# Regrouping the projection matmuls inside the slots of a sliding-window attention kernel

## The chip, the cores and the metric

The kernel runs on one core of a Trainium2 chip. The metric is the device time of one execution in microseconds (us). The core has five engines that run their own instruction streams and meet by semaphores: TensorE (PE in the profile, with its weight loads as PEld), VectorE (DVE), ScalarE (ACT), GpSimd (POOL) and SyncE (SP), which here issues the transfers. TensorE writes only PSUM, a small memory of banks with 512 floats per partition.

## The reference

Everything is float32, with 2048 tokens of width 512.

```python
xn = layernorm(x)
q, k, v = heads(xn @ wqkv)                      # 32 heads of 16
scores = q @ k.T * 16 ** -0.5                   # each query sees itself and the 255 keys before it
s = softmax(where(mask, scores, -1e9)) @ v @ wo
y = layernorm(xn)
g = silu(gelu(y @ w1 + b1) @ w2 + b2)           # 512 -> 1792 -> 512
out = x + s * g
```

## The kernel before

Numbers of full float32 precision are split into a high and a low part, and a product is made of three matmuls (`PASSES`: high by high, high by low, low by high).

The attention is a loop over *slots*, t = 0 to 127. The 32 heads form eight groups n of four heads, and a slot handles one block of 128 tokens of one group: n = t // 16, block t % 16. Each slot issues the following, and every engine keeps this order (`Ordered`; the order is written out by hand in the last loop of `mixer_kernel`, and no scheduler changes it):

1. `prob_block(..., 1)`: the scores of two of the four heads, two matmuls that run side by side on the two halves of TensorE's rows, into the PSUM tile `stb`. ScalarE then makes exp of them (`pt<-stb`), and GpSimd cuts out the window with two selects.
2. `max_block` for the block that lies `LEAD` = 12 slots ahead (m = t + 12): four matmuls into the tile `xy`, with the keys of the block before and of the block itself; VectorE puts in place of the masked part the scores with the keys two blocks back (`copy_predicated`, which reads `zo`), and takes the row maximum (`mt<-xy`). Those scores with the keys two blocks back are `first_scores`, four small matmuls into `zo`. They are made at the end of the slot before, unless `max_block` is told that they are not made ahead; it then makes them itself, straight after its own four.
3. *fills of the first half* (`fill_in(t, 0)`), then whatever `plan` has for the slot.
4. `prob_block(..., 0)`: the scores of the other two heads, again into `stb`. So `stb` has to be read by the exp of step 1 before these may start, and by the exp of step 4 before the next slot may start.
5. *fills of the second half* (`fill_in(t, 1)`), then `first_scores` of block m + 1 (none in slots with t % 16 = 3 or 4, since the first two blocks of a group have no keys two blocks back).
6. `pv_step` of the block before: 24 small matmuls with the probabilities of three blocks (8 in slots with t % 16 = 1, 16 in those with t % 16 = 2), into `zo`, and ScalarE's copy of the result, `oraw<-zo`.

From slot 116 on there is no block ahead, so steps 2 and the `first_scores` are gone, and step 1 writes `xy` in place of `stb`.

The *fills* are matmuls of other stages, put between the scores: the projection to q and k of the next group (`pair_qk`), to v (`pair_v`), and the hidden layer of the MLP (`pair_h`). `tandem(t0, t1, one, two, mid, back)` spreads two such jobs over the slots t0 to t1. A job is n units (12, or 24 half as long ones for `pair_v`); one unit of a *pair of fills* is one matmul on the upper 64 rows and one on the lower 64 rows, side by side, into the two banks `fb[0]` and `fb[1]`. The units go through the n steps twice: in phase 0 (slots t0 to mid - 1) the banks take one half of the rows, in phase 1 (from mid, or `back`, on) they change rows. At that change, the first pair of phase 1 is made to wait for the newest `oraw` copy (`add_manual_dep`). In slot t1 the last three units come, and the two banks are copied out: bank 0 by ScalarE, bank 1 by VectorE (`pjr<-fb`, `vt<-fb`, `hr<-fb`); the next tandem begins in the slot after.

`places` inside `tandem` says how many of a slot's units go in its first half: `ahead`, at most a third of n (four pairs), or half of the slot's units. `BEHIND` lists eight slots t1 in which ScalarE's copy of bank 0 comes in the second half, behind the second exp.

After the copies of a projection come the split (ScalarE casts the high part, GpSimd subtracts) and six transfers per job to the tiles `qk`, from which the scores are made (`send_high`, `send_low`, line 43 like all issued work, since one helper records every operation).

Of the kernel before, what the change touches and what calls it, by code (L numbers as in the profile page):

```python
# [23 lines left out]
NQ = H // 4  # L24
EPS = 1e-5
NEG = -3.0e38
LEAD = 12
# [23 lines left out]
def mixer_kernel(ctx, tc, x, wqk, wv, wo, w1, b1, w2, b2, out):  # L51


    nc = SimpleNamespace(**{name: Ordered(tc, name) for name in ("tensor", "vector", "scalar", "gpsimd", "sync")})
# [22 lines left out]
    def load(pool, tag, src, name, shape=(P, 512)):  # L77
        t = pool.tile(list(shape), F32, tag=tag, name=name)
        nc.sync.dma_start(t, src)
        return t  # L80
# [79 lines left out]
    def run(steps):  # L160
        for step in steps:
            step()
# [13 lines left out]
    def open_slot(i):  # L176
        slots.append(bigp.tile([P, 2, 2, S], F32R, tag=f"qk{i}", name=f"qk{i}"))
# [18 lines left out]
    fb = [psf.tile([P, 512], F32, name=f"fb{i}") for i in range(2)]  # L196
# [90 lines left out]
    now = [0, 0]  # L287
    delayed = {}
    fills = {}

    def later(k, fn):

        if k == 0:
            fn()
        else:
            h = 2 * now[0] + now[1] + k
            delayed.setdefault((h // 2, h % 2), []).append(fn)
# [137 lines left out]
                behind(t, nc.sync.dma_start, h_d[f - 6], raw)  # L435
        return 3 * KT, mm, finish

    BEHIND = (19, 24, 35, 41, 58, 74, 90, 104)

    def tandem(t0, t1, one, two, mid=None, back=None):  # L440

        n = one[0]
        lo, hi = slice(0, 64), slice(64, P)
        mid = mid or max(1, (t0 + t1 + 1) // 2)
        most = n // 4

        def places(slots, last):

            last = min(most, n // (len(slots) + 1)) if last else 0
            cuts = [(n - last) * k // len(slots) for k in range(len(slots) + 1)]
            out = []
            for t, a, b in zip(slots, cuts, cuts[1:]):
                ahead = min(b - a, max(n // 3, (b - a + 1) // 2))
                out += [(t, 0)] * ahead + [(t, 1)] * (b - a - ahead)
            return out + [(t1, 0)] * last

        first, second = places(range(t0, mid), False), places(range(back or mid, t1), True)
        for phase, where in enumerate((first, second)):  # L460
            for i in range(n):
                flags = dict(start=(phase == 0 and i == 0), stop=(phase == 1 and i == n - 1), skip_group_check=True)
                def unit(i=i, phase=phase, flags=flags):
                    made = ((two if phase == 0 else one)[1](fb[1 - phase], i, hi, **flags),
                            (one if phase == 0 else two)[1](fb[phase], i, lo, **flags))
                    if phase == 1 and i == 0:
                        for r in made:
                            tc.add_manual_dep(r.ins, outs["copy"].ins.name, ORDER, reason="the banks change rows")
                fills.setdefault(where[i], []).append((unit, ()))
        fills.setdefault((t1, int(t1 in BEHIND)), []).append((one[2], (fb[0], t1, nc.scalar.copy)))  # L470
        fills[t1, 0].append((two[2], (fb[1], t1, nc.vector.tensor_copy)))

    def spread(jobs, places):
# [13 lines left out]
    def first_scores(n, qb):  # L487

        slot = slots[n % 2]
        for p in range(2):  # L490
            for a in (1, 0):
                r = slice(64 * a, 64 * a + 64)
                nc.tensor.matmul(zo[:, a, P * p: P * (p + 1)], slot[r, 0, p, P * qb: P * (qb + 1)],
                                 slot[r, 1, p, P * (qb - 2): P * (qb - 1)], start=True, stop=True)

    def max_block(n, qb, ahead=False):

        slot = slots[n % 2]
        if qb % 4 == 0:
            mts[n, qb // 4] = small.tile([P, 2, 2, 4], F32, tag="mt", name=f"mt_{n}_{qb}")  # L500
        lo = max(qb - 1, 0)
        off = 128 * (lo + 1 - qb)
        for p in range(2):
            for a in (1, 0):
                r = slice(64 * a, 64 * a + 64)
                nc.tensor.matmul(xy[:, a, 256 * p + off: 256 * (p + 1)], slot[r, 0, p, P * qb: P * (qb + 1)],
                                 slot[r, 1, p, P * lo: P * (qb + 1)], start=True, stop=True)
        if qb >= 2 and not ahead:
            first_scores(n, qb)
        four = xy.rearrange("q a (p k) -> q a p k", p=2)  # L510
        nc.vector.copy_predicated(four[:, :, :, 128:256], mask,
                                  neg if qb < 2 else zo[:, :, 0:256].rearrange("q a (p k) -> q a p k", p=2))
        nc.vector.tensor_reduce(out=mts[n, qb // 4][:, :, :, qb % 4],
                                in_=four[:, :, :, off:256],
                                axis=AX.X, op=ALU.max, negate=True)
# [32 lines left out]
    def prob_block(n, kb, p):  # L548
        slot = slots[n % 2]
        w = min(384, S - P * kb)  # L550
        pt = pp.tile([P, 2, 384], F32, tag="pt", name=f"pt_{n}_{kb}_{p}")
        both = xy if p and 16 * n + kb + LEAD >= 16 * NQ else stb[0]
        for a in (1, 0):
            r = slice(64 * a, 64 * a + 64)
            nc.tensor.matmul(both[:, a, 0:w], slot[r, 1, p, P * kb: P * (kb + 1)],
                             slot[r, 0, p, P * kb: P * kb + w], start=True, stop=True)
        nc.scalar.activation(pt[:, :, 0:w], both[:, :, 0:w], AF.Exp, scale=DH ** -0.5)
        nc.gpsimd.affine_select(out=pt[:, :, 0:P], in_=pt[:, :, 0:P], pattern=[[0, 2], [1, P]],
                                compare_op=ALU.is_ge, fill=0.0, base=0, channel_multiplier=-1)
        if w == 384:  # L560
            nc.gpsimd.affine_select(out=pt[:, :, 256:384], in_=pt[:, :, 256:384],
                                    pattern=[[0, 2], [-1, P]], compare_op=ALU.is_gt, fill=0.0,
                                    base=0, channel_multiplier=1)
        pts[(n, kb, p)] = pt
# [100 lines left out]
    def at(t, fn, *args):  # L665
        plan.setdefault(t, []).append((fn, args))
# [8 lines left out]
    ahead = load(pp, "pt", x[512: 640, :], "x_1_0")  # L675
# [28 lines left out]
    n, raw = raws["qk"]  # L704
# [32 lines left out]
    fills[0, 1].insert(0, fills[0, 0].pop())  # L737
    soon = {}
    tandem(3, 8, pair_qk(1, 2), pair_qk(1, 3))
    for n, spans in enumerate((((9, 14), (15, 19)), ((20, 24), (25, 30)), ((31, 35), (36, 41)), ((42, 47), (48, 53, 51)),  # L740
                               ((75, 79), (80, 84)), ((85, 90), (93, 98))), 2):
        for c, span in zip((0, 2), spans):
            tandem(*span[:2], pair_qk(n, c), pair_qk(n, c + 1), *span[2:])
    for i, (t0, t1) in enumerate(((54, 58), (59, 63), (64, 68), (69, 74))):
        tandem(t0, t1, pair_v(2 * i), pair_v(2 * i + 1))
# [66 lines left out]
    def fill_in(t, half):  # L812
        now[:] = t, half
        run(delayed.pop((t, half), ()))
        for fn, args in fills.get((t, half), ()):
            fn(*args)

    end = 16 * NQ
    for t in range(-16, end + 1):
        m = t + LEAD  # L820
        if t == -5:
            open_slot(1)
            for k in range(4):
                at(-4 + k, clear_part, k)
        if 0 <= t < end:
            if t == 0:
                early.close()
                stb.append(attn.enter_context(tc.tile_pool(name="ps_s2", bufs=1, space=PSUM)).tile(
                    [P, 2, 512], F32, name="stb"))
            prob_block(t // 16, t % 16, 1)  # L830
        if t >= 0 and m < end:
            max_block(m // 16, m % 16, t > 0)
        fill_in(t, 0)
        for fn, args in plan.get(t, []):
            fn(*args)
        if 4 <= m < LEAD:
            max_block(0, m)
        if 0 <= t < end:
            prob_block(t // 16, t % 16, 0)
        fill_in(t, 1)  # L840
        if 0 <= m < 4:
            max_block(0, m)
        if t >= 0 and m + 1 < end and (m + 1) % 16 >= 2:
            first_scores((m + 1) // 16, (m + 1) % 16)
        if t >= 1:
            pv_step((t - 1) // 16, (t - 1) % 16)
        run(lns.get(t, ()))
        if 0 <= m < end and m % 4 == 3:
            max_rows(m // 16, m % 16 // 4, t)
        for fn, args in ends.get(t, []):  # L850
            fn(*args)
# [22 lines left out]
    for f in range(6, NF, 2):  # L874
        t = gp.tile([P, 2, 512], F32, tag="ohl", name=f"hr_{f}", bufs=4)
# [429 lines left out]
```

## Time and profile before

| | |
|---|---|
| median of three runs | 753.11 us (752.19 to 753.17) |
| the profiled execution | 751.99 us |
| its span, first to last instruction | 750.3 us |
| TensorE busy | 735.8 us, 98% of the span |
| VectorE, ScalarE, GpSimd busy | 511.3, 439.5, 299.1 us |
| granted TensorE clock | 0.999 |
| slots 0 to 115 | from 62.0 to 398.4 us |
| slots 116 to 127 | from 398.4 to 427 us |

The timeline view gives one row for each run of like instructions on an engine: start, duration from the first start to the last end, engine, operation, what is written and read, how many, and in brackets the idle time before it and who ended it. Durations of matmuls overlap: the next matmul starts before the one before has left the array, so the time that a matmul takes from TensorE is read from start to start. A slot begins at the first matmul of `stb` of step 1; its first half ends at the start of the second pair on `stb`, and its second half at the next slot's first.

### The profile page before, as it was taken

The page shows a single profiled execution, that of the slowest core. Times are in us where ns is not written, and L with a number is a line of the kernel's source. Part 1 is how long each engine was busy: PE and PEld are TensorE (multiplying, and loading weights), DVE is VectorE, ACT ScalarE, POOL GpSimd, SP SyncE. Part 2 cuts the span into 40 slices and gives each one's busy share as a digit, 9 for nine tenths or more (in the row PEclk, how much of TensorE's full clock was granted, in tenths as well). Part 3 has the DMA queues.
Part 4 walks back from the last instruction along what each step waited for, and adds up shares of the span by engine and source line. Part 5 has one row for each costly group of instructions (what it writes and reads, how often), then busy time and mean ns, then how long its engine had stood idle before and what let it go on. Part 6 is the DMA issues. An engine that isn't in the chain of part 4 may idle for free.

```text
span 750.3 us, 18757 instructions
## 1 busy us (share of the span) xinstructions
PE 735.8 (98%) x7408; PEld 589.3 (79%) x7408; DVE 511.3 (68%) x781; ACT 439.5 (59%) x746; POOL 299.1 (40%) x644
## 2 busy tenths in 40 slices
PE   8999999999999999999999999999999999999997
PEld 7886777777778887777776688888888888888886
DVE  7886767877766778887772547763666765676643
ACT  7757767867667676778877745544453743442001
POOL 7413757767666555767866600120102000001102
PEclk9999999999999999999999999999999999999999
DMA  8633355766555535647734482542013332254711
GB/s 287 191 74 78 84 132 148 210 153 187 150 142 148 143 93 139 168 109 189 200 86 146 120 294 92 177 147 78 35 43 98 94 103 71 70 167 129 214 53 56
DMA packets 56951, 99.40 MB, mean 132 GB/s; under 512 B 11104, under 2 KB 11360, under 8 KB 56864
## 3 DMA queue, kind: packets, MB, share of 16 engines
q1 hardware_dynamic: 56864, 98.21, 46.0%
q8 instruction: 58, 0.95, 0.5%
q14 instruction: 29, 0.24, 0.1%
HBM read 51.39 MB, written 29.62 MB: 108 GB/s over the span
## 4 chain that ended last, share of the span: by engine, by line
PE 90%; ACT 4%; DVE 3%; DMA 1%; issue 1%; POOL 0%; SPq 0%; DVEq 0%; ACTq 0%
PE acc L43 20%; PE fb L43 19%; PE zo L43 12%; PE stb L43 9%; PE p L43 9%; PE s L43 6%; PE h L43 6%; PE xy L43 5%; PE pv L43 3%; ACT pt L43 3%; DVE xy L43 1%; PE yt L43 1%; DVE mt L43 1%; DMA qk<-pjr 0%; DMA x<-in_x_dram 0%
## 5 line engine op out<-in xcount | busy, mean ns | idle before, releaser
L43 POOL TENSOR_SCALAR_AFFINE_SELECT pt<-pt 128x256 f32<-128x256 f32 x480 | 193.7, 427 | 134.2 <-ACT pt L43 131.9
L43 ACT ACTIVATE pt<-stb 128x768 f32<-128x768 f32 (+1 forms) x244 | 188.4, 772 | 58.4 <-PE stb L43 51.7
L43 DVE TENSOR_REDUCE mt<-xy 128x4 f32<-128x1024 f32 (+1 forms) x128 | 152.6, 1192 | 4.4
L43 DVE COPY_PREDICATED xy<-upper,zo 128x512 f32<-128x512 int32 x112 | 77.8, 694 | 71.5 <-PE xy L43 64.9
L43 PE MATMUL fb<-xnT,wqb 64*128 64x512 f32 (+1 forms) x684 | 106.9, 398 | 0.3
L43 POOL TENSOR_TENSOR xo<-xo,gated 128x512 f32<-128x512 f32 x15 | 20.3, 1354 | 216.6 <-DVE gated L43 191.5
L43 PE MATMUL zo<-pt,vt 128*17 128x128 f32 x2880 | 103.7, 275 | 0.1
L43 PE MATMUL stb<-qk 64*128 64x384 f32 (+1 forms) x488 | 98.9, 401 | 4.5 <-ACT pt L43 2.8
L43 PE MATMUL acc<-w,gh 128*128 128x512 f32 x320 | 98.9, 390 | 0.0
L43 PEld LDWEIGHTS stb<-qk 64*128 64x128 f32 x488 | 45.5, 183 | 53.3 <-ACT pt L43 45.1
L43 PEld LDWEIGHTS zo<-pt,vt 128*17 128x17 f32 x2880 | 67.5, 97 | 15.2 <-issue 6.5
L43 PEld LDWEIGHTS fb<-xnT,wqb 64*128 64x128 f32 (+1 forms) x684 | 64.2, 185 | 10.0 <-DVE pjr L43 1.1
L43 PEld LDWEIGHTS acc<-w,gh 128*128 128x128 f32 x320 | 59.8, 188 | 12.1
L43 PE MATMUL acc<-w,gl 128*128 128x512 f32 x160 | 62.4, 390 | 0.0
L43 PE MATMUL xy<-qk 64*128 64x256 f32 (+2 forms) x536 | 58.3, 291 | 0.2 <-DVE mt L43 0.2
L43 ACT COPY oraw<-zo 128x128 f32<-128x128 f32 x128 | 34.2, 267 | 35.9 <-PE zo L43 34.8
L43 PEld LDWEIGHTS xy<-qk 64*128 64x128 f32 x536 | 46.8, 185 | 6.5 <-issue 3.1
L43 ACT ACTIVATE gated<-acc 128x512 f32<-128x512 f32 x16 | 8.7, 596 | 64.8 <-DVE acc L43 64.8
L43 PE MATMUL s<-wos,ohl 128*128 128x512 f32 (+1 forms) x204 | 44.7, 377 | 0.0
L43 PEld LDWEIGHTS zo<-qk 64*128 64x128 f32 x448 | 38.4, 185 | 6.0 <-issue 2.5
L43 PEld LDWEIGHTS s<-wos,ohl 128*128 128x128 f32 x204 | 36.7, 188 | 7.0
L43 ACT COPY p<-p 128x512 f32<-128x512 f32 x21 | 12.3, 584 | 49.5 <-PE p L43 42.2
(195 smaller groups left out, 1243.2 us busy)
## 6 DMA issues: line engine op xcount, KB each, us to landing
qk<-sh SPq DMA_DIRECT2D x128, 128.0 KB
qk<-pjr SPq DMA_DIRECT2D x64, 128.0 KB
oT_d<-oraw SPq DMA_DIRECT2D x32, 256.0 KB
w_d<-in_w_dram SPq DMA_DIRECT2D x14, 512.0 KB
x<-in_x_dram SPq DMA_DIRECT2D x16, 256.0 KB
or<-oT_d SPq DMA_DIRECT2D x16, 256.0 KB
w<-rden_d SPq DMA_DIRECT2D x16, 256.0 KB
xo<-in_x_dram SPq DMA_DIRECT2D x16, 256.0 KB
```

Of the source, the lines that this page charges most:

```text
L43: r = issue(*args, **kwargs)
```

## The change

Four edits to the order of work; no arithmetic, no tile and no transfer is added or removed.

- `places`: before slot 116, up to 5n/12 units of a slot (five pairs, or ten of the half-length units) go into its first half, whatever number the slot has. From slot 116 on it is a quarter of n (three), or half of the slot's units.
- The wait at the change of rows is not made in tandems that begin in slot 116 or later. There are two of them, which change rows in slots 119 and 125.
- `BEHIND` is gone: ScalarE's copy of bank 0 always comes in the first half of slot t1, ahead of the second exp, and its tiles are taken before those of VectorE's copy.
- `IN_PLACE`: the `first_scores` of the blocks m = 12 and m = 24 are made within `max_block`, in slots 0 and 12. For m = 12 that was so before (`t > 0` was false in slot 0); for m = 24 they move from the end of slot 11 to the first half of slot 12.

```diff
@@ -287,6 +287,7 @@
     fills = {}
+    IN_PLACE = (LEAD, 24)
@@ -435,8 +436,6 @@
-    BEHIND = (19, 24, 35, 41, 58, 74, 90, 104)
-
     def tandem(t0, t1, one, two, mid=None, back=None):
@@ -452,7 +451,7 @@
             for t, a, b in zip(slots, cuts, cuts[1:]):
-                ahead = min(b - a, max(n // 3, (b - a + 1) // 2))
+                ahead = min(b - a, 5 * n // 12) if t < 16 * NQ - LEAD else min(b - a, max(most, (b - a + 1) // 2))
                 out += [(t, 0)] * ahead + [(t, 1)] * (b - a - ahead)
@@ -463,11 +462,11 @@
-                    if phase == 1 and i == 0:
+                    if phase == 1 and i == 0 and t0 < 16 * NQ - LEAD:
                         for r in made:
                             tc.add_manual_dep(r.ins, outs["copy"].ins.name, ORDER, reason="the banks change rows")
                 fills.setdefault(where[i], []).append((unit, ()))
-        fills.setdefault((t1, int(t1 in BEHIND)), []).append((one[2], (fb[0], t1, nc.scalar.copy)))
+        fills.setdefault((t1, 0), []).append((one[2], (fb[0], t1, nc.scalar.copy)))
         fills[t1, 0].append((two[2], (fb[1], t1, nc.vector.tensor_copy)))
@@ -829,7 +828,7 @@
         if t >= 0 and m < end:
-            max_block(m // 16, m % 16, t > 0)
+            max_block(m // 16, m % 16, m not in IN_PLACE)
@@ -840,7 +839,7 @@
-        if t >= 0 and m + 1 < end and (m + 1) % 16 >= 2:
+        if t >= 0 and m + 1 < end and (m + 1) % 16 >= 2 and m + 1 not in IN_PLACE:
             first_scores((m + 1) // 16, (m + 1) % 16)
```

## The prediction

> **What bounds the kernel now.** I began with the page: TensorE is busy for 98% of the span, the others for 68% and less. Then the waits, to see what breaks into TensorE's stream.
>
> ```profile
> span 750.3 us, 18757 instructions
> PE 735.8 (98%) x7408; PEld 589.3 (79%) x7408; DVE 511.3 (68%) x781; ACT 439.5 (59%) x746; POOL 299.1 (40%) x644
> ...
> PEld stb L43 <- ACT pt L43: 45.1, 161, 0.7
> ```
>
> The last row says that the weight load for a score pair (`stb`) waits for ScalarE's exp 161 times. There is one tile `stb` and two exps per slot, so a slot has two lower bounds side by side: TensorE's own work, and the loop score, exp, score. The timeline of slot 13, which has four pairs of fills in its first half and one in its second (4+1), shows both.
>
> ```profile
> 100.84 0.44 PE L43 MATMUL stb<-qk 64*128 64x384 f32 x2
> 101.12 0.39 PE L43 MATMUL xy<-qk 64*128 64x256 f32 x4
> 101.35 1.09 PE L43 MATMUL fb<-xnT,wqb 64*128 64x512 f32 x8
> 102.28 0.43 PE L43 MATMUL stb<-qk 64*128 64x384 f32 x2
> 102.55 0.39 PE L43 MATMUL fb<-xnT,wqb 64*128 64x512 f32 x2
> ...
> 103.83 0.39 PE L43 MATMUL stb<-qk 64*128 64x256 f32 x2
> ...
> 102.76 0.81 ACT L43 ACTIVATE pt<-stb 128x768 f32<-128x768 f32 x1 [0.54 <-PE stb L43]
> ```
>
> Read from start to start: a score pair takes 0.28 us (100.84 to 101.12), four pairs of fills 0.93 (101.35 to 102.28), so a pair 0.235. The slot takes 2.99: a first half of 1.44 and a second of 1.55. The second exp ends at 103.57, 0.26 before the next slot, so this second half is TensorE's. It is not so in slot 18, also 4+1, where `pv_step` has 16 matmuls in place of 24:
>
> ```profile
> 115.78 0.44 PE L43 MATMUL stb<-qk 64*128 64x384 f32 x2 [0.39 <-ACT pt L43]
> 117.21 0.42 PE L43 MATMUL stb<-qk 64*128 64x384 f32 x2
> 118.54 0.46 PE L43 MATMUL stb<-qk 64*128 64x384 f32 x2
> ```
>
> It takes 2.76, with halves of 1.43 and 1.33: its fifth pair costs nothing, since it lies under the exp.
>
> **The change, part by part. Five pairs in the first half.** I worked the cuts of `places` through for all tandems. Before slot 116, 42 slots change: 4+1 becomes 5+0, 4+2 becomes 5+1, and some `pair_v` slots gain half a pair. With a fifth pair the first half is TensorE's: 0.51 up to the first fill (100.84 to 101.35) and five times 0.235, 1.69. What the second half becomes needs a slot in which the first exp is done long before the second score. Slot 42 (4+0) is one, because its fills began late:
>
> ```profile
> 184.98 0.45 PE L43 MATMUL stb<-qk 64*128 64x384 f32 x2
> ...
> 186.61 0.33 PE L43 MATMUL stb<-qk 64*128 64x384 f32 x2
> 186.78 0.33 PE L43 MATMUL zo<-qk 64*128 64x128 f32 x4
> ...
> 187.85 0.45 PE L43 MATMUL stb<-qk 64*128 64x384 f32 x2
> ...
> 186.41 0.19 PEld L43 LDWEIGHTS stb<-qk 64*128 64x128 f32 x2
> ...
> 186.99 0.81 ACT L43 ACTIVATE pt<-stb 128x768 f32<-128x768 f32 x1 [0.63 <-PE stb L43]
> ```
>
> The weight load of the score starts at 186.41, 0.20 before its matmul, under the last fills. So the pair takes 0.17 (186.61 to 186.78) and not 0.28, its exp starts 0.38 behind it and not 0.48, and the second half is 1.24, which is now the least a second half with a full exp can have (0.38 + 0.81 + 0.05 to the next score).
>
> - *Slots like 13* (7, 13, 23, 40, 89, 103, 109): 2.99 becomes 1.69 + 1.24 = 2.93. With the slots a little shorter than 13, 0.05 each, -0.35 for seven. Slot 29, of the same kind, I leave at 0.
> - *Slots like 18*, whose second half was already the exp's (18, 34, 52, 83, 97, 114, and 65 and 81, which have 4+2 but 8 matmuls of `pv_step`): 2.76 becomes 2.93, +0.17 each, +1.36 for eight. Two slots of `pair_v` (66, 67) move half a pair; by slot 18's price I estimate +0.1 each: +0.2.
> - *4+2 becoming 5+1*, slot 16:
>
> ```profile
> 109.82 0.44 PE L43 MATMUL stb<-qk 64*128 64x384 f32 x2
> ...
> 111.28 0.40 PE L43 MATMUL stb<-qk 64*128 64x384 f32 x2
> 111.52 0.63 PE L43 MATMUL fb<-xnT,wqb 64*128 64x512 f32 x4
> ...
> 113.03 0.44 PE L43 MATMUL stb<-qk 64*128 64x384 f32 x2
> ```
>
> TensorE's work binds both halves and the pair only moves; what is gained is the rest of the load, 0.24 (111.28 to 111.52) down to 0.17: -0.06 or a little more. Seven slots (16, 21, 32, 55, 60, 76, 112), -0.45. In nine others the first half starts late behind the bank copies, so that the load is hidden already: 0. Three slots with short exps (46, 62, 78): 0. Five `pair_v` slots with half a pair (56, 57, 61, 72, 73): -0.07.
>
> Sum of the fills: -0.35 + 1.36 + 0.2 - 0.45 - 0.07 = **+0.7**. Taken alone this edit is a loss: it moves the pair away from the exp that hid it.
>
> No trace of before shows five pairs in a first half. The bounds: if no load gets hidden, the 30 slots not yet hidden keep 0.28 in place of 0.17, +3.3; if the eight slots like 18 lose nothing, -1.4. I take neither, as slot 42 is nearest.
>
> The Trainium skill, "TensorE: Matmul & The Clock Gate", says in the section "The mechanism" of its Part 3 that LDWEIGHTS overlaps with matmuls in flight only where their row groups differ. Scores and fills both hold both halves of the rows, so by that sentence the fifth pair would hide nothing and the sum would be 3.3 higher; the load at 186.41, under fills, disagrees. I go by the trace.
>
> **First scores in slot 12.** Slots 11 and 12:
>
> ```profile
> 94.34 0.44 PE L43 MATMUL stb<-qk 64*128 64x384 f32 x2
> ...
> 95.80 0.39 PE L43 MATMUL stb<-qk 64*128 64x384 f32 x2
> 96.91 0.44 PE L43 MATMUL zo<-qk 64*128 64x128 f32 x4 [0.72 <-DMA qk<-pjr]
> 97.28 0.85 PE L43 MATMUL zo<-pt,vt 128*17 128x128 f32 x24
> 98.06 0.44 PE L43 MATMUL stb<-qk 64*128 64x384 f32 x2
> ```
>
> At 96.91 TensorE waits for a transfer of the projection, with `pv_step`'s 24 matmuls queued behind. Without it the second half of slot 11 (95.80 to 98.06, 2.26) is the exp's: with 0.38 to 0.48 from score to exp it is 1.24 to 1.34, and I take 1.30. That is -0.96. In slot 12 the four matmuls of `xy` read the same columns and inherit the wait, but are due at 97.10 + 0.28 = 97.38, 0.47 after the landing. The four of `zo` now stand in the first half. What they cost there, an early block shows:
>
> ```profile
> 59.90 0.34 PE L43 MATMUL zo<-qk 64*128 64x128 f32 x4
> 60.16 0.96 PE L43 MATMUL fb<-xnT,wqb 128*128 128x512 f32 x3
> ```
>
> 0.26, less 0.05 for the load that becomes hidden. Sum: -0.96 + 0.21 = **-0.75**. Slot 0 does not change.
>
> **No wait at the last change of rows.** Slots 119 and 125:
>
> ```profile
> 405.67 0.44 PE L43 MATMUL xy<-qk 64*128 64x384 f32 x2
> 406.53 0.50 PE L43 MATMUL fb<-yh,xnT 64*128 64x512 f32 x2 [0.42 <-ACT oraw L43]
> ...
> 420.21 0.45 PE L43 MATMUL xy<-qk 64*128 64x384 f32 x2
> 420.85 0.50 PE L43 MATMUL fb<-yh,xnT 64*128 64x512 f32 x2 [0.20 <-ACT oraw L43]
> ...
> 405.51 0.81 ACT L43 ACTIVATE pt<-stb 128x768 f32<-128x768 f32 x1
> ```
>
> From a score to the next matmul 0.28 is needed; here it is 0.86 and 0.64. So 0.58 and 0.36 go, and the first pair, whose load the wait laid bare (0.50 long against 0.39 at 102.55), gets 0.11 shorter each time. What is late next in slot 119: three fills, then the score on `stb` at 405.95 + 0.70 = 406.65, whose tile is free at 405.51 + 0.81 = 406.32. It holds: **-1.15**. The other late edit, three and three units in place of four and two, shifts 0.235 from half to half. There TensorE binds and the exps alternate between `xy` and `stb`, which covers it: 0. Without that cover it would be +0.24 in each of eight slots.
>
> **Bank copies in the first half.** Slot 8 has ScalarE's copy first already, slot 19 has it behind:
>
> ```profile
> 87.19 0.59 ACT L43 COPY pjr<-fb 128x512 f32<-128x512 f32 x1
> 87.70 0.81 ACT L43 ACTIVATE pt<-stb 128x768 f32<-128x768 f32 x1
> ...
> 121.16 0.58 ACT L43 COPY pjr<-fb 128x512 f32<-128x512 f32 x1
> ...
> 121.21 0.68 DVE L43 COPY pjr<-fb 128x512 f32<-128x512 f32 x1
> 121.99 1.17 PE L43 MATMUL fb<-xnT,wqb 64*128 64x512 f32 x8
> ```
>
> The next tandem's first pair needs both banks, and VectorE's copy (to 121.89) ends after ScalarE's (121.74) even when that comes late. So nothing is won. In slot 8 the copy fits between the two exps. If the last fill came late, the exp behind the copy would slip by at most the 0.59. I take **0** for the eight. The split's cast, GpSimd's subtraction and the order of transfers on SP's queue stay; only the buffers that the copies get are taken in another order.
>
> **Sum.** 0.7 - 0.75 - 1.15 + 0 = -1.2. On the profiled execution (751.99 us, span 750.3) that is 750.8; on the median of the three runs (753.11, 1.1 above the profiled one), **751.9**. Behind the attention TensorE runs on without a break, so the end moves with it. What a measurement of this kernel can tell is about 0.2%, 1.5 us: the forecast lies just inside.
>
> **Rivals.**
> - *Slower: no load is hidden.* Place: the second score of 30 slots. Price +3.3, so -1.2 + 3.3 = +2.1: 755.2. It decides from about 0.09 us per slot upwards (30 x 0.09 = 2.7, the time then 1.5 above). For it: ordinarily the load does wait (161 times). Against it: 186.41.
> - *The wait for the transfer only moves.* If the transfer lands more than 0.47 later, `xy` in slot 12 stops TensorE as `zo` did: the 0.75 are lost, 752.7. Against it: transfer and slot are shifted alike by what goes before (slot 7, 0.05).
> - *Faster: the slots like 18 lose nothing*, because the five pairs leave the exp more room than slot 42 shows: -1.2 - 1.4 = -2.6, 750.5. Against it: the 1.24 of slot 42 is one full exp and its two latencies.
>
> **How the numbers follow.** Forecast 0.62, with an error of some 0.6 from forty terms of a few hundredths: half of it beyond 1.5 us faster, half within. Slower rival 0.14, transfer 0.12 (within), faster rival 0.12. So faster 0.31 + 0.12 = 0.43, same 0.31 + 0.12 = 0.43, slower 0.14. The range, from the faster rival's 750.5 to past the transfer's 752.7 by the spread of the runs (0.9): 750.3 to 753.6, leaves out the slower rival and little else.
>
> **What would show it.** Right: slot 13 at 2.93 and slot 18 at 2.93; score loads 0.2 ahead of their matmuls; no idle TensorE before `zo` in slot 11; in slots 119 and 125 fills 0.28 behind `xy`. Wrong: second halves behind five pairs of 1.35 or more, a wait for the transfer before `xy` in slot 12, or exps that slip behind the bank copies.

## The result, and the profile after

| | before | after |
|---|---|---|
| median | 752.3 us (752.0 to 753.17, 11 runs) | 750.86 us (750.55 to 751.3, 11 runs) |
| the profiled execution, its span | 751.99, 750.3 us | 750.88, 749.2 us |
| ratio of the medians | | 0.9978, 95% interval 0.9969 to 0.9988 |

The changed kernel is 1.44 us faster by the medians, 0.22%, and the interval excludes a ratio of 1. The forecast was 751.9, a move of -1.2.

The page of after: its span and busy line, and from the waits the row of the score's weight load.

```profile
span 749.2 us, 18758 instructions
PE 733.9 (98%) x7408; PEld 590.4 (79%) x7408; DVE 511.7 (68%) x781; ACT 441.1 (59%) x746; POOL 299.3 (40%) x644
...
PEld stb L43 <- ACT pt L43: 46.6, 159, 0.7
```

TensorE still bounds the kernel at 98%, and its busy time fell by 1.9 us (735.8 to 733.9) with the same 7408 matmuls. The load of `stb` waits for ScalarE 159 times in place of 161, for 46.6 us in place of 45.1. So the page as a whole tells little of this change; it has to be read slot by slot.

The timeline of after, slot 13 and the start of slot 14, TensorE first, then its weight loads and ScalarE:

```profile
100.00 0.44 PE L43 MATMUL stb<-qk 64*128 64x384 f32 x2
...
100.50 1.32 PE L43 MATMUL fb<-xnT,wqb 64*128 64x512 f32 x10
101.66 0.34 PE L43 MATMUL stb<-qk 64*128 64x384 f32 x2
101.84 0.34 PE L43 MATMUL zo<-qk 64*128 64x128 f32 x4
...
102.91 0.39 PE L43 MATMUL stb<-qk 64*128 64x256 f32 x2
...
101.44 0.19 PEld L43 LDWEIGHTS stb<-qk 64*128 64x128 f32 x2
...
102.05 0.81 ACT L43 ACTIVATE pt<-stb 128x768 f32<-128x768 f32 x1 [0.67 <-PE stb L43]
```

Five pairs stand in the first half (x10). The second score's weights are loaded at 101.44, 0.22 ahead of its matmul; the score pair takes 0.18 (101.66 to 101.84), its exp starts 0.39 behind it, and the second half lasts 1.24 (101.66 to 102.91). The slot takes 2.91 in place of 2.99. All of it is slot 42 of before over again.

Slot 18 of after, which lost:

```profile
114.77 0.44 PE L43 MATMUL stb<-qk 64*128 64x384 f32 x2 [0.35 <-ACT pt L43]
...
115.29 1.32 PE L43 MATMUL fb<-xnT,wqb 64*128 64x512 f32 x10
116.45 0.33 PE L43 MATMUL stb<-qk 64*128 64x384 f32 x2
...
117.69 0.45 PE L43 MATMUL stb<-qk 64*128 64x384 f32 x2 [0.17 <-ACT pt L43]
```

It takes 2.92 (114.77 to 117.69) in place of 2.76: its second half is 1.24 too, with TensorE idle before the next score, since the pair that used to fill this time has gone to the first half.

Slots 11 and 12 of after, with the issue of the two transfers of the projection on SP's queue:

```profile
95.63 0.40 PE L43 MATMUL stb<-qk 64*128 64x384 f32 x2
95.96 0.85 PE L43 MATMUL zo<-pt,vt 128*17 128x128 f32 x24
96.93 0.44 PE L43 MATMUL stb<-qk 64*128 64x384 f32 x2
97.27 0.50 PE L43 MATMUL xy<-qk 64*128 64x256 f32 x4
...
92.50 1.18 SPq L43 DMA_DIRECT2D qk<-pjr  x2
```

`pv_step` no longer stands behind `zo`: the second half of slot 11 is 1.31 (95.63 to 96.93) in place of 2.26. In slot 12 `xy` comes 0.34 behind its score, where 0.28 is usual.

Slots 119 and 124 of after, and GpSimd's selects around them. A run of like instructions is one row, and the last one is cut where the view ends, at 420.2 us, just after VectorE's work beside it ends (420.0).

```profile
405.29 0.44 PE L43 MATMUL xy<-qk 64*128 64x384 f32 x2
405.57 0.39 PE L43 MATMUL fb<-yh,xnT 64*128 64x512 f32 x2
...
418.03 0.63 PE L43 MATMUL zo<-pt,vt 128*17 128x128 f32 x16
418.98 0.41 PE L43 MATMUL zo<-pt,vt 128*17 128x128 f32 x8 [0.31 <-POOL pt L43]
419.32 0.44 PE L43 MATMUL xy<-qk 64*128 64x384 f32 x2
419.60 0.40 PE L43 MATMUL fb<-yh,xnT 64*128 64x512 f32 x2
...
405.30 3.06 POOL L43 TENSOR_SCALAR_AFFINE_SELECT pt<-pt 128x256 f32<-128x256 f32 x8 [1.15 <-ACT pt L43]
...
412.67 7.61 POOL L43 TENSOR_SCALAR_AFFINE_SELECT pt<-pt 128x256 f32<-128x256 f32 x11 [0.43 <-ACT pt L43]
```

The fills of slots 119 and 125 now come 0.28 behind `xy` (405.57, 419.60); both waits are gone. But in slot 124 `pv_step` breaks off for 0.31 and waits for the probabilities (`pt`) that GpSimd cuts out. A select, which takes 0.38 at 405 (3.06 for eight), takes 0.69 there (7.61 for eleven).

Where the time went, by slot lengths read from start to start in both traces (the account ends at the second score of slot 127):

| | us |
|---|---|
| 42 slots with a changed cut | +0.35 |
| eight slots with a moved bank copy | -0.01 |
| slots 11 and 12 | -0.68 |
| second score of slot 115 to that of slot 127 (29.22 to 28.23) | -0.99 |
| other slots (slot 107 alone -0.16), and the start 0.12 earlier | -0.04 |
| behind slot 127 (324.05 to 324.30) | +0.25 |
| sum, as the spans (750.28 to 749.16) | -1.12 |

### The profile page after: what moved, and what is told of

The parts are those of the page before. It is cut to its first block, busy times and chain, and to the rows that moved or that the text cites. A ratio compares the mean times of both kernels' runs of the same rounds, so it can differ in the third digit from the quotient of the medians.

```text
span 749.2 us, 18758 instructions
## 1 busy us (share of the span) xinstructions
PE 733.9 (98%) x7408; PEld 590.4 (79%) x7408; DVE 511.7 (68%) x781; ACT 441.1 (59%) x746; POOL 299.3 (40%) x644
## 4 chain that ended last, share of the span: by engine, by line
PE 89%; ACT 5%; DVE 2%; POOL 2%; issue 1%; DMA 1%; SPq 0%; DVEq 0%; ACTq 0%; POOLq 0%
PE acc L43 20%; PE fb L43 18%; PE zo L43 11%; PE stb L43 9%; PE p L43 9%; PE s L43 6%; PE h L43 6%; PE xy L43 5%; ACT pt L43 4%; PE pv L43 3%; POOL pt L43 1%; DVE xy L43 1%; PE yt L43 1%; DMA x<-in_x_dram 1%; DVE mt L43 0%
## 5 line engine op out<-in xcount | busy, mean ns | idle before, releaser
L43 PE MATMUL fb<-xnT,wqb 64*128 64x512 f32 (+1 forms) x684 | 104.8, 397 | 0.3
L43 PE MATMUL stb<-qk 64*128 64x384 f32 (+1 forms) x488 | 97.2, 393 | 6.2 <-ACT pt L43 4.1
L43 PEld LDWEIGHTS stb<-qk 64*128 64x128 f32 x488 | 45.8, 183 | 51.6 <-ACT pt L43 46.6
```

The source lines that it names most:

```text
L43: r = issue(*args, **kwargs)
```

## The experiments

Four kernels first, each before with one part of the change alone. They ran on one chip beside runs of before with a median of 752.17.

**Fills alone.**

```diff
-                ahead = min(b - a, max(n // 3, (b - a + 1) // 2))
+                ahead = min(b - a, 5 * n // 12) if t < 16 * NQ - LEAD else min(b - a, max(n // 3, (b - a + 1) // 2))
```

> Only the cut of the fills before slot 116 (up to five pairs in a first half). Theory: in slots whose second half TensorE binds it gains 0.05 to 0.08 us, in the eight whose second half is the exp's it loses about 0.15, in two by half of that; summed over the slots +0.35 to +0.7 us, so 0.05 to 0.1% slower than before. Rival (the five pairs are where the gain comes from): 0.5 us or more faster than before.

Measured: 752.69, ratio 1.0007 (0.9998 to 1.0016). By time that is +0.5, not to be told from nothing. In its trace the changed slots lengthen by 0.36 in sum, as in after. Its span is 1.0 longer than that of before, and 0.63 of it is slot 11, which this edit doesn't touch. The timeline of this kernel, the transfers' issue and the matmuls that read them:

```profile
92.66 1.17 SPq L43 DMA_DIRECT2D qk<-pjr  x2
...
97.54 0.44 PE L43 MATMUL zo<-qk 64*128 64x128 f32 x4 [1.35 <-DMA qk<-pjr]
```

And the same issue in the trace of before, whose `zo` was at 96.91:

```profile
92.66 1.17 SPq L43 DMA_DIRECT2D qk<-pjr  x2
```

Issued at the same 92.66, the transfer is waited for 0.63 longer in this execution. I come back to that below.

**First scores in place, alone.**

```diff
+    IN_PLACE = (LEAD, 24)
...
-            max_block(m // 16, m % 16, t > 0)
+            max_block(m // 16, m % 16, m not in IN_PLACE)
...
-        if t >= 0 and m + 1 < end and (m + 1) % 16 >= 2:
+        if t >= 0 and m + 1 < end and (m + 1) % 16 >= 2 and m + 1 not in IN_PLACE:
```

> Only the first scores of block 24 moved into slot 12. Theory: -0.7 us (slot 11 about 2.76 us long in place of 3.72, slot 12 about 3.05 in place of 2.78). Rival (the wait for the transfer only moves): no change, with idle time of TensorE before xy in slot 12.

Measured: 751.15, 0.9989 (0.998 to 0.9998). Slot 11 loses 0.96 as predicted, slot 12 gets 0.31 longer.

**The late slots alone** (no wait, and three and three units).

```diff
-                ahead = min(b - a, max(n // 3, (b - a + 1) // 2))
+                ahead = min(b - a, max(n // 3 if t < 16 * NQ - LEAD else most, (b - a + 1) // 2))
...
-                    if phase == 1 and i == 0:
+                    if phase == 1 and i == 0 and t0 < 16 * NQ - LEAD:
```

> Only the two edits from slot 116 on: no wait at the change of rows, and three and three units in place of four and two. Theory: -1.0 us: slot 119 gives 0.68, slot 125 some 0.46 of which GpSimd's selects take back 0.2 in slot 124. Rival: by GpSimd's backlog less than half of that is kept, -0.5 us or less.

Measured: 751.39, 0.9988 (0.9979 to 0.9997). The stretch from slot 115 to 127 is 1.02 shorter (28.20), as in after and less than the 1.15 predicted.

**Bank copies alone.**

```diff
-        fills.setdefault((t1, int(t1 in BEHIND)), []).append((one[2], (fb[0], t1, nc.scalar.copy)))
+        fills.setdefault((t1, 0), []).append((one[2], (fb[0], t1, nc.scalar.copy)))
```

> Only ScalarE's copies of bank 0 moved into the first half in all tandems. Theory: 0, within 0.2 us by the slots' lengths, since VectorE's copy is the later one. Rival: the second exp of these slots slips by up to 0.3 us each, eight times: up to +2.4 us; or the next tandem starts earlier by 0.1 each, -0.8 us.

Measured: 752.34, 1.0001 (0.9992 to 1.0009). The eight slots differ by 0.005 in sum: nothing.

The four differences of medians (+0.52, -1.02, -0.78, +0.17) sum to -1.11; each is uncertain by about 0.7. The parts add, then, as far as this can tell. What was open was whether the fills are a loss that could be avoided, and what takes back part of the late gain.

**After without the new cut of the fills** (before's cut up to slot 115).

```diff
-                ahead = min(b - a, 5 * n // 12) if t < 16 * NQ - LEAD else min(b - a, max(most, (b - a + 1) // 2))
+                ahead = min(b - a, max(n // 3 if t < 16 * NQ - LEAD else most, (b - a + 1) // 2))
```

> The changed kernel without its cut of the fills before slot 116 (four pairs in a first half, as in the kernel before); the other three edits stay. Theory: the fills cost 0.4 to 0.7 us, so this is faster than the changed kernel by that: -1.7 to -2.1 us against the kernel before. Rival (the fills carry part of the gain together with the other edits): slower than the changed kernel, -1.2 us or less against the kernel before.

Measured: 750.26, 0.9975 (0.9966 to 0.9984). The changed slots are 0.32 shorter than in after. By time that can't be told from after's 0.9978, but the sign agrees with the fills alone.

**The fifth pair only where TensorE binds the second half.** The ten slots that I had counted as losing keep four pairs.

```diff
+    STAY = (18, 34, 52, 65, 66, 67, 81, 83, 97, 114)
...
-                ahead = min(b - a, 5 * n // 12) if t < 16 * NQ - LEAD else min(b - a, max(most, (b - a + 1) // 2))
+                ahead = min(b - a, 5 * n // 12 if t not in STAY else n // 3) if t < 16 * NQ - LEAD else min(b - a, max(most, (b - a + 1) // 2))
```

> The changed kernel with the old cut in the ten slots 18, 34, 52, 65, 66, 67, 81, 83, 97 and 114, whose second half was the exp's. Theory: their losses (1.4 us summed over the slots of the changed kernel) go and the gains (0.9) stay: -2.6 us against the kernel before, 1.3 faster than the changed kernel. Rival (the sum of the slots is not kept to the end): no faster than the changed kernel by more than 0.5 us.

Measured: 749.14, 0.9962 (0.995 to 0.9975); span 747.4. Slot 18 of this kernel:

```profile
114.70 0.45 PE L43 MATMUL stb<-qk 64*128 64x384 f32 x2 [0.35 <-ACT pt L43]
115.22 1.09 PE L43 MATMUL fb<-xnT,wqb 64*128 64x512 f32 x8
116.15 0.41 PE L43 MATMUL stb<-qk 64*128 64x384 f32 x2
116.40 0.39 PE L43 MATMUL fb<-xnT,wqb 64*128 64x512 f32 x2
117.47 0.44 PE L43 MATMUL stb<-qk 64*128 64x384 f32 x2
```

It is back at 2.77, and the ten slots together are 1.39 shorter than in after. So the same move wins in one kind of slot and loses in the other, by which resource ends the second half.

**Six pairs.**

```diff
-                ahead = min(b - a, 5 * n // 12) if t < 16 * NQ - LEAD else min(b - a, max(most, (b - a + 1) // 2))
+                ahead = min(b - a, 6 * n // 12) if t < 16 * NQ - LEAD else min(b - a, max(most, (b - a + 1) // 2))
```

> Six pairs allowed in a first half before slot 116, so 5+1 becomes 6+0 in sixteen slots and nothing else moves against the changed kernel. Theory (the second half cannot be shorter than 1.24 when its exp is a full one): such a slot goes from 1.67 + 1.46 to 1.90 + 1.24, +0.02 to +0.03, and in the slots 20, 65 and 81, whose second half is at 1.24 to 1.28 already, +0.2; in 15, 31 and 111, with short exps, 0. In all +0.6 to +1.0 us against the changed kernel. Rival (no such floor; the pair only moves): no change against the changed kernel.

Measured: 751.75, 0.9995 (0.9986 to 1.0004). Eighteen slots get another cut than in after (I had counted sixteen); together they are 1.14 longer. Slot 112 of this kernel:

```profile
387.33 0.45 PE L43 MATMUL stb<-qk 64*128 64x384 f32 x2
387.85 1.56 PE L43 MATMUL fb<-xnT 64*128 64x512 f32 x12
389.24 0.34 PE L43 MATMUL stb<-qk 64*128 64x384 f32 x2
390.48 0.44 PE L43 MATMUL stb<-qk 64*128 64x384 f32 x2
```

The first half is 1.91 for six pairs; the second, now without a fill, is 1.24 (389.24 to 390.48). With one fill in it, it was 1.45 in after, 0.21 longer; a pair takes 0.235. So in such slots the sixth pair only moves (here +0.02), and where the second half stood at 1.25 already it is a plain loss (slot 65 +0.25, slot 81 +0.24). Slot 20, with a second half of 1.28, lost 0.34, more than the 0.2 that I had given it. The 1.24 is the floor that the prediction took from slot 42.

Now the late slots. My theory was that GpSimd's selects run slow beside VectorE's work on `w2` (a cast and a subtraction for each of seven tiles, issued from slot 121 on), and that this makes `pv_step` wait in slot 124; the rival was that the earlier slot 119 alone makes the probabilities late.

The timeline of after, VectorE: two of the rows that follow on one another from 411 to 420 us.

```profile
415.87 0.62 DVE L43 CAST w<-w 128x512 fp32r<-128x512 f32 x1
416.53 0.78 DVE L43 TENSOR_TENSOR w<-w 128x512 fp32r<-128x512 f32 x1
```

**VectorE's work on `w2` in other slots** (after, with one line changed).

```diff
-        at(121 + f, settle, "w2", f, by_vector, nc.vector)
+        at((119, 119, 120, 125, 125, 126, 126)[f], settle, "w2", f, by_vector, nc.vector)
```

> The changed kernel with VectorE's splits of w2 moved from the slots 121 to 127 to the slots 119, 119, 120, 125, 125, 126, 126. Theory (in the slots 121 to 124 GpSimd's selects are stretched from 0.41 to 0.58 and 0.85 us by VectorE's work beside them, and TensorE waits for them in slot 124): selects of 0.41 in the slots 122 to 124, no idle time of TensorE in slot 124, 0.4 us faster than the changed kernel. Rival (GpSimd is late for another reason): the wait in slot 124 stays, no change.

Measured: 750.09, 0.9975 (0.9967 to 0.9984); span 748.3. The timeline of this kernel, TensorE in slot 124, GpSimd (its rows cut where the views end, at 417.2 and at 421 us), and VectorE's last instruction of this stretch:

```profile
417.83 0.85 PE L43 MATMUL zo<-pt,vt 128*17 128x128 f32 x24
418.71 0.44 PE L43 MATMUL xy<-qk 64*128 64x384 f32 x2
...
412.47 4.91 POOL L43 TENSOR_SCALAR_AFFINE_SELECT pt<-pt 128x256 f32<-128x256 f32 x7 [0.43 <-ACT pt L43]
418.73 2.35 POOL L43 TENSOR_SCALAR_AFFINE_SELECT pt<-pt 128x256 f32<-128x256 f32 x6 [0.27 <-ACT pt L43]
...
416.34 0.77 DVE L43 TENSOR_TENSOR w<-w 128x512 fp32r<-128x512 f32 x1
```

Three of the seven tiles were done early, at 399 to 403, and four still ran from 411.6 to 417.1. So the edit did not clear the whole stretch, but VectorE now ends before slot 124. While it runs a select takes 0.70 (4.91 for seven), behind it 0.39 (2.35 for six). `pv_step` no longer breaks off: from its start to the next `xy` it is 0.88 in place of 1.29, and from the second score of slot 124 to that of 125 it is 2.12 in place of 2.53. In time the kernel can't be told from after (0.9975 to 0.9978).

**Only the wait taken out.**

```diff
-                    if phase == 1 and i == 0:
+                    if phase == 1 and i == 0 and t0 < 16 * NQ - LEAD:
```

> The kernel before without the wait at the change of rows in the slots 119 and 125, four and two units as before. Theory (the wait is all of the late gain, the split of the units nothing): the same as with both late edits, -0.9 us. Rival (three and three units are needed, since the second score of slot 119 would else be late): 0.3 us or more less.

**Only the late split, three and three.**

```diff
-                ahead = min(b - a, max(n // 3, (b - a + 1) // 2))
+                ahead = min(b - a, max(n // 3 if t < 16 * NQ - LEAD else most, (b - a + 1) // 2))
```

> The kernel before with three and three units in place of four and two from slot 116 on, the wait kept. Theory: 0, within 0.1 us between the slots 115 and 127. Rival: the earlier second exps take GpSimd's lag out of slot 124, -0.3 us; or the exps are in the way, +0.24 us in each of eight slots.

Measured: without the wait 751.29, 0.999 (0.9981 to 1.0); with the split alone 752.17, 1.0 (0.999 to 1.0009), against 752.27. Slots 119 and 124 without the wait:

```profile
405.95 0.44 PE L43 MATMUL xy<-qk 64*128 64x384 f32 x2
406.23 0.40 PE L43 MATMUL fb<-yh,xnT 64*128 64x512 f32 x2
...
418.67 1.18 PE L43 MATMUL zo<-pt,vt 128*17 128x128 f32 x24
419.78 0.44 PE L43 MATMUL xy<-qk 64*128 64x384 f32 x2
```

The same two slots with the split alone:

```profile
406.17 0.44 PE L43 MATMUL xy<-qk 64*128 64x384 f32 x2
407.03 0.50 PE L43 MATMUL fb<-yh,xnT 64*128 64x512 f32 x2 [0.42 <-ACT oraw L43]
...
419.61 0.63 PE L43 MATMUL zo<-pt,vt 128*17 128x128 f32 x16
420.55 0.41 PE L43 MATMUL zo<-pt,vt 128*17 128x128 f32 x8 [0.30 <-POOL pt L43]
420.89 0.44 PE L43 MATMUL xy<-qk 64*128 64x384 f32 x2
421.35 0.50 PE L43 MATMUL fb<-yh,xnT 64*128 64x512 f32 x2
...
420.33 0.81 ACT L43 ACTIVATE pt<-stb 128x768 f32<-128x768 f32 x1
```

ScalarE's exp of the same score in before:

```profile
419.83 0.81 ACT L43 ACTIVATE pt<-stb 128x768 f32<-128x768 f32 x1
```

My rival falls: with the wait gone and slot 119 early, `pv_step` of slot 124 takes 1.11 to the next `xy` (418.67 to 419.78), as in before (419.10 to 420.21). With the split alone it takes 1.28, with slot 119 still late. So it is the split that lengthens this stretch, by 0.17. By the single records of the two traces, the first select that starts in slot 122 takes 0.85 with the split, in place of 0.66, and the next one starts 1.42 behind the slot's start, in place of 1.25. Part of the delay was there before: without VectorE beside it the same stretch was 0.88. Without the split the stretch from slot 115 to 127 is 1.22 shorter, with it 1.02. The split alone changes that stretch by only 0.01, since slot 125 gives back what slot 124 loses. There the fill waits for the `oraw` copy, which stands on ScalarE behind the exp shown: the fill starts 1.02 behind the start of that exp in both traces (419.83 to 420.85 in before, 420.33 to 421.35 here). A later `xy` only takes from that wait (0.64 from `xy` to fill in before, 0.46 here). So the split is free as long as the wait is there, and costs 0.20 once it is gone.

**Both mends together**: the fifth pair only where TensorE binds, and the `w2` work moved.

> Both improvements on the changed kernel: the old cut in the ten slots whose second half is the exp's, and VectorE's splits of w2 out of the slots 121 to 124. Theory (the two lie at different places on the same chain and add up): -1.6 and -0.5 us, so 2.1 us faster than the changed kernel, -3.6 us against the kernel before. Rival (a wait further on takes it back): less than -3.1 us, no better than the ten slots alone.

Measured: 748.8 against 752.27, 0.9957 (0.9943 to 0.9971). This is the best version: 3.5 us faster than before, and by the spans 2.1 faster than after (747.1 in place of 749.2). It keeps what the change won, and drops the loss in the ten slots and the wait in slot 124.

## Why the prediction was right, and where its terms were off

The forecast move was -1.2; the medians moved by 1.44, the spans by 1.1. The time of 751.9 was 1.0 too high, and 0.8 of it is the base: the move was added to the median of three runs, 753.11, and eleven runs of before have 752.3. From there -1.2 would have been 751.1. The prediction took 1.5 us for the least that can be told from no change; the result's interval is 0.7 us to either side, so a move of -1.2 could already be told.

The mechanisms were right in the main (the split of the late slots was not), but that the sums agree so well is in part luck. By the profiles the fills cost 0.35 less than predicted, the late slots won 0.16 less and slots 11 and 12 0.07 less, and these errors cancel in part. The last of them hangs on one landing of a transfer, which spreads by more than all of them, as shown below.

**Fills: +0.7 predicted, +0.35 measured.** The mechanism was right throughout: the load hides (101.44), the second half is 1.24, slot 13 is 2.91 and slot 18 is 2.92 where 2.93 was said for both. The sum was mis-sized by many small amounts, nearly all of one sign: the seven slots like 13 gave -0.40 (-0.35 predicted), the eight like 18 +1.22 (+1.36), the two of `pair_v` +0.16 (+0.2), the seven 4+2 slots -0.54 (-0.45), the nine with the load already hidden -0.05 (0), and the rest -0.04 (-0.07). I had priced the eight by slot 18, at 2.76 one of the shortest before; slots 97 and 83, at 2.78 and 2.80, lost 0.12 and 0.13. And the first half that I put at 1.69 came out at 1.66 to 1.68 in six of the eight.

This disposes of two rivals. "No load is hidden" would have left slot 13's second half at 1.35; it is 1.24. The Trainium skill, "TensorE: Matmul & The Clock Gate", section "The mechanism" of its Part 3, was named for that rival, with its sentence that weight loads overlap with matmuls in flight only where the row groups differ; the load at 101.44, under fills that hold the same rows, disagrees with that sentence as the load at 186.41 did. "The slots like 18 lose nothing" falls with slot 18's 2.92.

**First scores in slot 12: -0.75 predicted, -0.68 in the profile.** Slot 11 was exact (-0.96). Slot 12 cost 0.28, not 0.21. The step that failed is the margin: the transfer was to land 0.47 before `xy` needs it, and `xy` comes 0.06 late in after (0.34 behind its score). That rival, "the wait only moves", came true in a small part. The margin was taken from one landing, and it was an early one, which also means that before usually waited longer than its profile shows. In the five experiments that leave slot 11 as it was, TensorE's idle time before `zo` was 1.09 to 1.35, against 0.72 in the profile that I predicted from. The other traces show what that does to the gain: slots 11 and 12 together take 6.50 in before and 6.88 to 7.13 in those five, and 5.80 to 5.95 in the seven kernels that move the scores. The means are 6.93 and 5.84, so over these executions the part is worth about 1.1, not 0.68 or 0.75. This fits the kernel with this part alone (-1.02 by medians).

The rival was also mispriced. It took the whole 0.75 for lost when the transfer lands later; but a later landing lengthens slot 11 of before as well, and in the seven kernels `xy` comes only 0.04 to 0.18 late.

**Late wait: -1.15 predicted, -0.99 measured.** The term itself was right: with only the wait taken out, slot 119 is 0.70 shorter and slot 125 0.49, together 1.2. What failed is the sentence on the split of three and three, "there TensorE binds and the exps alternate, which covers it: 0". I had asked only for TensorE and the exps; `pv_step` also waits for GpSimd's selects, which in slots 122 to 124 run at little more than half their pace beside VectorE (0.69 in place of 0.38). With the split its wait in slot 124 is 0.17 longer. The 0 held for the split with the wait kept (0.01), and failed with the wait gone.

**Copies: 0 predicted, 0 measured**, in after (-0.01) and alone (0.00).

Two more differences between the two profiles are chance and not the change. Slot 107 was 2.95 in the profile of before and is 2.79 to 2.80 in all twelve others, also where this slot is as before. The stretch behind slot 127, 0.25 longer in after, is 324.00 to 324.08 in ten of the eleven experiments, those with all of the late edits among them; the one without the wait has 324.53. So the end moves with the attention, as the prediction said, within such a scatter.

## What to carry to other kernels

A piece of filling work is worth moving only out of a stretch that its own engine ends; in a stretch that another engine's latency ends it was free, and a rule that moves it everywhere gives back what it wins. Find the floor of such a stretch in one slot of the trace that happens to show it, and price each slot against it. For a step costed at nothing, go through all engines that the next consumer waits for, not only the two that bound the loop.

## What the runs showed of the hardware

- GpSimd's select on 128x256 floats takes 0.38 to 0.39 us when VectorE is idle and 0.69 to 0.70 us beside VectorE's cast and subtraction on 128x512 (rows above, duration by count). One by one in after, a select that starts under a subtraction takes 0.85, and one that starts under a cast 0.59. The Trainium skill, "GPSIMD Engine Reference", section "8. Key points", says that GpSimd shares its SBUF interfaces with VectorE and meets contention from VectorE's instructions in a 2-port perf mode or with two SBUF inputs; the subtraction has two such inputs, and the paces agree with that.
- The same pair of 128 KB transfers, issued at the same 92.66 us in two executions, was waited for until 96.91 and until 97.54. A margin of less than this 0.63 behind such a transfer, read from one profile, is no margin.
- A weight load goes ahead of its matmul under running fills (0.22 us, slot 13 of after), but the load of a score behind the small matmuls of `pv_step` does not: in 114 of the slots 1 to 115 of before, and in as many of after, it starts with its matmul. In the timeline of before, slot 14's load starts with the score, at 103.83, although the exp that it has to wait for ended at 103.57:

```profile
103.83 0.19 PEld L43 LDWEIGHTS stb<-qk 64*128 64x128 f32 x2 [0.21 <-ACT pt L43]
```
